# Eight transfers instead of three in a loop that this data never enters, and where the last store's semaphore comes to lie

## The chip, the core and the metric

The kernel runs on one core of a Trainium2 chip. TensorE (PE) multiplies matrices into PSUM and takes its weights on a track of its own (PEld); VectorE (DVE) and ScalarE (ACT) work element by element; GpSimd (POOL) does some copies and issues the software transfers; SyncE (SP) computes nothing and issues transfers and waits. The engines run apart and meet at semaphores. The metric is the device time of one execution in microseconds.

## The reference

```python
scores = scale * np.matmul(q, k.transpose(0, 1, 3, 2))      # batch 8, 8 heads, 576 positions, 64 wide
mask = (rel >= 0) & (rel < window)                           # window 64, causal
attn = softmax(np.where(mask, scores, -1000000000.0))
x = matmul(attn, v), heads side by side                      # 4608 tokens x 512
out = (silu(x @ w_gate) * (x @ w_val)) @ w_out               # 512 -> 1536 -> 512
```

Each position sees itself and the 63 before it. The attention's output goes straight into a gated feed-forward block.

## The kernel before

The 4608 tokens are worked in nine tiles of 512. A tile is the first 512 positions of one batch; the eighth tile gathers the last 64 positions of all eight batches. For each tile the kernel computes scores, their exponentials and the sums, mixes the values, scales into `xT`, runs twelve slices of gate and value products into `hT` (`gate_value`, L469), and projects `hT` in four parts of 128 tokens (`project_part`, L479). The order is written out by hand: the tile framework here only places the semaphores, so each engine's instructions come in the order of the source. The projections of one tile are woven between the attention of the next.

This fast path leaves out the maximum in the softmax. That is right as long as no sum gets out of bounds, so it gathers evidence as it goes: `survey` (L542) and `tally` (L549) count the partitions whose sums stayed in range into `count`. Near the end (L984) every engine loads that number as `good`, and behind it stands a general path for the data that the fast path can't do:

```python
with tc.If(good < P, preferred_fallthrough_block=True):      # L990
    set_exp()
    with tc.For_i(0, 8 * H, 1) as i:                         # L992
        general_attention(i)
    set_silu()
    with tc.For_i(0, NTOK // P, 1) as i:                     # L995
        general_ffn(i)
project(NT - 1, 2, bank[4])                                  # L997
project_last(NT - 1, 3)                                      # L998
```

The first loop does the attention of one head of one batch per turn, the second the feed-forward block for 128 tokens per turn. They write all of the output anew. Parts 0 and 1 of the last tile are projected ahead of the `If`, parts 2 and 3 behind it. With the data given here all sums stay in range, `good` is 128, and both loops are skipped.

Three things matter around the change:

Behind the `If` SyncE issues three stores: part 2 of the last tile (`project_end`, L513, 256 KB), and part 3 in two pieces of 384 and 128 columns (`project_last`, L540, 192 KB and 64 KB). The 64 KB store is the last of the kernel. Before, these three have hardware semaphores 0, 1 and 2.

## Time and profile before

| | us |
|---|---|
| median of 3 runs | 322.56 (322.48 to 322.86) |
| profiled execution | 322.44 |
| its span, first to last instruction | 320.6 |
| granted TensorE clock | 1.000 |
| TensorE busy | 315.5 (98%) |
| last store issued | 317.66 to 318.05 |

The span runs from the program's first instruction to its last; 1.84 us of the execution's time lie around it. A share of 98% for TensorE means that elsewhere only the ends, where TensorE has not begun or is done, are open to change. In answers on a line, an instruction of an engine's sequencer (a semaphore wait, a branch, a drain) carries a `q` behind the engine's name; such an answer gives the count, the shortest, median and longest duration in nanoseconds, and the starts of the first and the last in microseconds.

### The profile page before, as it was taken

What the parts mean: (1) busy time and instruction counts of PE and PEld (TensorE: products, weight loads), DVE (VectorE), ACT (ScalarE), POOL (GpSimd) and SP (SyncE); (2) the same over time, 40 slices, a digit from 0 to 9 for tenths busy, and PEclk for the clock granted to TensorE, in tenths of its full rate; (3) what the DMA queues carried; (4) which work ended last, traced back from release to release, by engine and by line L of the source; (5) the groups of instructions that cost most, each with busy time, mean ns of one, the idle gap of its engine ahead of it and who ended that gap; (6) DMA issues with size and microseconds to landing.
All of it is one profiled execution on the core that took longest, in us unless ns stands there. A gap on an engine that the chain in (4) does not pass through costs nothing. (4 is left out here: it accounts for less than half of the span.)

```text
span 320.6 us, 8214 instructions
## 1 busy us (share of the span) xinstructions
PE 315.5 (98%) x3298; PEld 154.8 (48%) x3298; DVE 214.4 (67%) x349; ACT 208.7 (65%) x327; POOL 147.4 (46%) x268
## 2 busy tenths in 40 slices
PE   8999999999999999999999999999999999999995
PEld 3544444445444644455445544554446444644443
DVE  5879846497576847685688667866786576843431
ACT  5967665768565875688477946694667665875600
POOL 4965657767566235741751099408765300000000
PEclk9999999999999999999999999999999999999999
DMA  7999999999799449983994369629998400021012
GB/s 250 203 196 198 207 151 226 207 197 123 155 194 182 48 108 173 199 88 99 163 195 52 81 110 116 70 54 141 184 187 104 109 0 0 4 82 52 1 37 99
DMA packets 83529, 40.45 MB, mean 126 GB/s; under 512 B 64160, under 2 KB 78752, under 8 KB 83488
## 3 DMA queue, kind: packets, MB, share of 16 engines
q0 software_dynamic: 51488, 22.59, 58.6%
q1 hardware_dynamic: 31456, 16.79, 22.6%
q8 instruction: 26, 0.43, 0.6%
q10 hardware_dynamic: 544, 0.52, 0.5%
q14 instruction: 15, 0.12, 0.1%
HBM read 53.02 MB, written 9.44 MB: 195 GB/s over the span
## 5 line engine op out<-in xcount | busy, mean ns | idle before, releaser
L466 ACT ACTIVATE sg<-one 128x512 f32<-128x512 f32 x107 | 63.9, 597 | 80.6 <-PE one L473 67.8
L467 DVE TENSOR_TENSOR hT<-sg,one 128x512 bf16<-128x512 f32 x107 | 74.0, 692 | 57.4 <-PE one L473 53.8
L473 PE MATMUL one<-xT,wg 128*128 128x512 bf16 x416 | 106.8, 379 | 0.0
L473 PE MATMUL one<-xT,wv 128*128 128x512 bf16 x416 | 106.8, 379 | 0.0
L142 POOL DMA_DIRECT2D k_s<-in_k_dram x112 | 60.4, 560 | 27.0 <-DMA q_s<-in_q_dram 13.1
L473 PEld LDWEIGHTS <-wv 128*128 128x128 bf16 x416 | 40.7, 98 | 49.1
L473 PEld LDWEIGHTS <-wg 128*128 128x128 bf16 x416 | 40.6, 98 | 48.8
L482 PE MATMUL one<-wo,hT 128*128 128x512 bf16 x252 | 56.6, 380 | 0.1
L958 POOL COPY past<-xT 128x1 bf16<-128x1 bf16 x8 | 1.5, 189 | 87.6 <-DVE xT L430 87.5
L494 PE MATMUL one<-wo,hT 64*64 64x512 bf16 x672 | 40.0, 377 | 0.0
L482 PEld LDWEIGHTS <-hT 128*128 128x128 bf16 x252 | 23.7, 98 | 29.7 <-issue 2.6
L430 DVE TENSOR_TENSOR xT<-two,r 128x512 bf16<-128x512 f32 x34 | 21.3, 684 | 23.0 <-ACT r L353 23.0
L233 DVE STREAM_TRANSPOSE kT<-k_s 128x512 bf16<-128x512 bf16 x28 | 36.1, 1290 | 0.0
L755 ACT ACTIVATE eb<-eb 128x960 bf16<-128x960 bf16 (+1 forms) x32 | 32.1, 1002 | 0.0
L308 ACT ACTIVATE eb<-two 128x960 bf16<-128x960 f32 (+1 forms) x32 | 29.5, 974 | 3.0 <-PE two L293 2.9
L494 PEld LDWEIGHTS <-hT 64*64 64x64 bf16 x672 | 18.6, 107 | 13.6
L313 DVE TENSOR_TENSOR eb<-eb,mask 128x960 bf16<-128x960 bf16 (+1 forms) x32 | 20.9, 655 | 5.8 <-ACT eb L308 5.8
L223 DVE STREAM_TRANSPOSE qT<-q_s 128x512 bf16<-128x512 bf16 x32 | 22.2, 700 | 0.1
L353 ACT ACTIVATE r<-r 128x1024 f32<-128x1024 f32 (+1 forms) x20 | 19.2, 968 | 0.1
L318 DVE TENSOR_TENSOR both<-eb 128x512 bf16<-128x512 bf16 x32 | 13.6, 425 | 1.1
L168 POOL DMA_DIRECT2D vb<-in_v_dram x16 | 11.0, 701 | 6.6 <-DMA wo<-in_moe_w_out_dram 3.8
L107 POOL DMA_DIRECT2D q_s<-in_q_dram x24 | 13.0, 552 | 2.0 <-DMA v<-in_v_dram 1.3
(149 smaller groups left out, 273.1 us busy)
## 6 DMA issues: line engine op xcount, KB each, us to landing
k_s<-in_k_dram POOLq DMA_DIRECT2D x112, 56.0 KB, 5.2
q_s<-in_q_dram POOLq DMA_DIRECT2D x24, 248.0 KB, 6.2
v_f<-in_v_dram SPq DMA_DIRECT2D x40, 128.0 KB
wg<-in_moe_w_gate_dram POOLq DMA_DIRECT2D x5, 256.0 KB, 8.3
wv<-in_moe_w_val_dram POOLq DMA_DIRECT2D x5, 256.0 KB, 8.9
q_f<-in_q_dram SPq DMA_DIRECT2D x4, 256.0 KB
wo<-in_moe_w_out_dram POOLq DMA_DIRECT2D x2, 512.0 KB, 10.7
vb<-in_v_dram POOLq DMA_DIRECT2D x16, 64.0 KB, 6.5
```

The costliest lines, as they stand in the source:

```text
L142: nc.gpsimd.dma_start(k_s[p0:p0 + 32, g, :, 0:w], k[b, a:H:2, s:s + P].rearrange("u (r e) d -> r u (e d)", e=4) [:, :, 32 * c:32 * c + w],)
L223: nc.vector.transpose(queries[t][:, u, :].rearrange("r (e x) -> r e x", e=16), staged[t][0][:, u].rearrange("r (e d) -> r e d", d=D)[:, :, ...
L233: nc.vector.transpose(dst[:, u, :].rearrange("r (g x e) -> r g e x", g=4, e=4), k_s[:, :, u].rearrange("r g (e d) -> r g e d", d=D)[:, :, ...
L308: nc.scalar.activation(flat, s_ps[:].rearrange("r a b -> r (a b)")[:, 0:n], AF.Exp, scale=0.125)
L313: nc.vector.tensor_mul(flat, flat, mask[:].rearrange("r j c e y -> r (j c e y)")[:, 0:n])
L430: nc.vector.tensor_mul(x, o_ps, r)
L466: nc.scalar.activation(sg[:], g_ps[:], AF.Silu)
L467: nc.vector.tensor_mul(hT[t][:, m, :], sg[:], v_ps[:])
L473: nc.tensor.matmul(ps[:], w[:, c, P * m:P * m + P], xT[t][:, c, :], start=(c == 0), stop=(c == 3),)
L482: nc.tensor.matmul(o_ps[:], hT[t][:, c, P * s:P * s + P], wo[:, c, :], start=(c == 0), stop=(c == 11),)
L494: nc.tensor.matmul(tiles[s][half(y)], hT[t][half(x), c, r0:r0 + 64], wo[half(x), c, :], start=not back and c == 0, stop=bool(back) and c = ...
L755: nc.scalar.activation(flat, flat, AF.Copy, accum_out=extent())
```

## The change

In `general_ffn`, the body of the second loop, the load of `x_b` is cut into four, one for each 128 rows of `x_all`, and each of the two stores is cut into two halves of the columns. That makes eight transfers on ScalarE's queue in the loop's text instead of three. What they move is the same. The semaphores are handed on from there: the three stores behind the `If` have hardware semaphores 5, 6 and 7 instead of 0, 1 and 2, so that the last has the eighth.

```diff
@@ general_ffn
         x_b = att.tile([P, 4, P], BF16, name="x_b", tag="xT")
-        nc.scalar.dma_start(
-            x_b[:], x_all[:, bass.ds(i * P, P)].rearrange("(c r) s -> r c s", r=P)
-        )
+        for c in range(4):
+            nc.scalar.dma_start(x_b[:, c], x_all[P * c:P * c + P, bass.ds(i * P, P)])
@@
         nc.scalar.copy(os_[:], bank[4])
-        nc.scalar.dma_start(out[bass.ds((i * P + NTOK - 64) % NTOK, 64)], os_[0:64])
-        nc.scalar.dma_start(out[bass.ds(i * P, 64)], os_[64:P])
+        ahead = (i * P + NTOK - 64) % NTOK
+        for f in (slice(0, 256), slice(256, 512)):
+            nc.scalar.dma_start(out[bass.ds(ahead, 64), f], os_[0:64, f])
+            nc.scalar.dma_start(out[bass.ds(i * P, 64), f], os_[64:P, f])
```

In the built program this changes, on the path that is executed: the amounts that the eight steps of the branch add (32 for all eight semaphores, where five had 16), the semaphores of the three stores, the number of waits ahead of the first of them on SyncE (three instructions instead of two), and the thresholds of the epilogue's waits. In the skipped part, SyncE's text has 12 instructions more and ScalarE's ten more.

Lines behind the loop body (from L664 on) are numbered one higher in the changed kernel: the `If` is L991, the epilogue L1024.

## The prediction

> **What bounds the kernel now.** I read the page first, for the engine shares and the chain, then the timeline of SyncE over the last microseconds, then the instructions of the epilogue's line and of the `If`'s line, and last the instruction packets. The page's head says that TensorE is the bound, and nowhere else can much be won or lost:

> ```profile
> PE 315.5 (98%) x3298; PEld 154.8 (48%) x3298; DVE 214.4 (67%) x349; ACT 208.7 (65%) x327; POOL 147.4 (46%) x268
> ```

> The lines of the changed loop (L632 to L663) have no instruction in the trace: the data are tame, `good` is 128, and every engine takes the branch over both loops. So the added transfers are never issued. What is left of the change is what the built program does with it on the executed path. The built programs agree instruction for instruction, semaphore and threshold up to the `If`; they differ only in the skipped second loop and in SyncE's tail behind the `If`. I therefore read that tail.

> The timeline of SyncE (start, duration, line, the store):

> ```profile
> 315.42 0.35 SPq L513 DMA_DIRECT2D out_dram<-os__4885  x1
> 317.24 0.81 SPq L540 DMA_DIRECT2D out_dram<-os__4888  x2
> ```

> The instructions of L1023 (the epilogue) on SyncE, asked of four short windows in order of time (count, min/median/max ns, first and last start):

> ```profile
> L1023 SPq EVENT_SEMAPHORE  x5: 17/28/28, 318.1 to 318.3; - x5
> ...
> L1023 SPq EVENT_SEMAPHORE  x1: 28/28/28, 319.2 to 319.2; - x1
> ...
> L1023 SPq EVENT_SEMAPHORE  x1: 28/28/28, 319.4 to 319.4; - x1
> ...
> L1023 SPq EVENT_SEMAPHORE  x5: 28/28/28, 319.4 to 319.7; - x5
> ```

> And the same line's drains, which come behind those waits, with SyncE's waits in the stretch from 318 to 321 us:

> ```profile
> L1023 SPq DRAIN  x2: 7/7/7, 319.7 to 319.8; - x2
> ```
> ```profile
> SPq L1023 <- DMA out_dram<-os__4888: 1.0, 2, 0.8
> ```

> Here is the epilogue. SyncE waits for the transfer queues' semaphores one instruction after another, in a fixed order: the eight software ones, paired, then hardware 0, 1, 2 ... 7, then a drain, then the barrier. There are twelve such waits. Before, the three stores behind the `If` carry hardware semaphores 0, 1 and 2. The first five waits pass at once (318.1 to 318.3; the fifth holds hardware 0). The sixth (hardware 1, the 192 KB store) is answered at 319.2, the seventh (hardware 2, the 64 KB store, the kernel's last) at 319.4. Then hardware 3 to 7 are still to be read, though they were full long ago: five waits, 319.4 to 319.7, and only then the drain. The reader should see that these five stand behind the last landing, on the path that ends the kernel.

> The other engines do not set the barrier:

> ```profile
> L1023 POOLq DRAIN  x1: 2682/2682/2682, 306.8 to 306.8; - x1
> L1023 ACTq DRAIN  x1: 8/8/8, 306.8 to 306.8; - x1
> L1023 PEldq DRAIN  x1: 1835/1835/1835, 315.4 to 315.4; - x1
> L1023 DVEq DRAIN  x1: 330/330/330, 317.3 to 317.3; - x1
> ```

> All four are drained by 317.6 us (317.3 + 0.33), 2.1 us before SyncE arrives.

> **The change part by part.**

> *The order of the hardware semaphores.* The three stores behind the `If` move from semaphores 0, 1, 2 to 5, 6, 7. The twelve waits stay, in the same order. Hardware 0 to 5 now pass while the two last stores are still on their way; hardware 6 is answered at 319.2, hardware 7 at 319.4, and the drain follows at once. So five waits leave the path. One costs 0.06 us from start to start: four such steps lie between 318.1 and 318.3, and five waits and the step to the drain fill 319.4 to 319.7. Bounds: the busy time alone is 5 x 28 ns = 0.14 us; by the rounded starts the stretch is at most 0.4 us. I take 5 x 0.06 = 0.30 us, the middle of the stretch itself. Moving five waits ahead of the landing costs nothing while they fit in the 0.8 us that SyncE waited there: 5 x 0.06 = 0.30 us, so 0.5 us of cover remains.

> [...]

> *One wait more ahead of the 256 KB store (L513).* SyncE's waits there go from two to three instructions, because that store now follows five semaphores instead of three. All are already full. They are covered:

> ```profile
> L990 SPq EVENT_SEMAPHORE  x4: 17/17/17, 314.7 to 314.9; - x4
> L513 SPq EVENT_SEMAPHORE  x2: 17/22/28, 315.0 to 315.0; - x2
> ```

> The store itself starts at 315.42, held by VectorE's copy of the same tile (314.70 + 0.69 = 315.39). One more step of 0.06 ends near 315.1, with 0.3 us to spare. Without that cover it would cost 0.06 us on this store alone, and the next store starts at 317.24, held by VectorE again (316.65 + 0.56 = 317.21). So nothing either way.

> *The eight semaphore steps on the branch not taken into the loops (L990).* They add 32 instead of 16 for five semaphores; same instructions, same waits. The fifth waits for the 256 KB store issued at 312.47 (answered at 314.7) before and after. Nothing.

> *Longer skipped code.* SyncE skips 12 instructions more (five in the block for no iteration, seven at the loop's back edge), ScalarE ten more; TensorE, VectorE and GpSimd skip what they did. Fetched code is a rival below. In the sum it is nothing: ScalarE's step behind the branch starts at 306.7, and TensorE, which waits for it, gets there at 311.83, 5.1 us later; SyncE's branch at 312.9 is followed by four waits from 313.1 to 313.4 and then by 1.3 us of waiting for the landing at 314.7. A delay of a microsecond at either branch would be swallowed.

> *Sum.* Profiled execution: 322.44 us (span 320.6, 1.84 around it) - 0.30 = 322.14. That execution stands 0.12 under the median of the three runs, 322.56; against the median: 322.56 - 0.30 = **322.26 us**, 0.09% less. About 0.2% (0.65 us) is what a measurement of this kernel can tell from no change, so by that bound this is no change: even the upper bound of 0.4 us stays inside, and the lower, 0.14, gives 322.42.

> **The rivals.**

> *Slower: a code boundary comes to lie in the tail.* The longer skip moves SyncE's last 35 instructions 12 places on. Code comes in packets on the instruction queues:

> ```profile
> q8 instruction: 26, 0.43, 0.6%
> ...
> q14 instruction: 15, 0.12, 0.1%
> ```

> A packet of q14 takes about 0.001 x 16 x 320.6 / 15 = 0.34 us (0.2 to 0.5 by the rounding), of q8 about 1.2. In a window of 306 to 309 us, 40 slices of 0.075 us, the packets stand at 307.3 and 308.8:

> ```profile
> DMA  0000000000000000070000000000000000000900
> ```

> That is 1.1 us behind the branches of ScalarE and GpSimd (306.2) and of TensorE (307.7). So a stall for code would be up to 1.1 + 0.34 = 1.4 us. It decides only where the boundary falls among the instructions behind the last landing: the drains and the two barrier steps. Then the time is 322.26 + 1.4 = 323.7 (for a packet alone 322.6). Ahead of 319.2 the wait for the stores covers it. Against it: all streams cross such boundaries some forty times (26 + 15 packets), TensorE is 98% busy through its own, and SyncE's first step behind its taken branch comes 0.2 us later (312.9 to 313.1), so the target was there already. For it: I can't see where SyncE's boundary lies. [...] Chance 0.12.

> *Nothing won: the barrier is held by something other than SyncE's arrival.* Then 322.56. Against it: the four drains above are over by 317.6, and the barrier's steps follow SyncE's drain at 319.8 directly. Chance 0.10.

> *The two last stores land in the other order.* The 64 KB store could be answered first; then one wait stays behind the last landing, and 4 x 0.06 = 0.24 is won: 322.32. It lands in the likeliest case's own range, and I count it there.

> *Faster by more.* The mirror of the first: the stall for code lies today behind the last instruction, within the 1.84 us outside the span, and goes: 322.26 - 1.4 = 320.9. No row shows such a stall. Chance 0.08.

> *The change doesn't do what it says.* That would need the last store on another semaphore; the built program puts it on the eighth. Excluded.

> **How the numbers follow.** Likeliest (0.70): 322.26, between 322.42 and 322.16 by the bounds, give or take the runs' own spread of about 0.2 (322.48 to 322.86). Nothing won 0.10, boundary 0.12, faster by more 0.08. The range holds the first two with that spread, 321.9 to 322.8, and leaves the other two out. Within 0.2%: 0.70 + 0.10 = 0.80. Slower 0.12, faster 0.08.

> **What would show it.** In the trace of the changed kernel: SyncE's twelve epilogue waits with ten of them started by 318.7, one at about 319.2 and one at about 319.4, and the first drain right behind at about 319.4 instead of 319.7; three waits of L513 behind the branch, with the store still at 315.4; a span of 320.3. The L540 stores should start at 317.2 as before. The prediction is wrong if the waits behind the last landing are still five, if the gap comes back between drain and barrier, or if a packet of q14 stands ahead of a gap on SyncE behind 319.4.

## The result, and the profile after

The changed kernel takes 322.10 us in the median of 22 runs (321.62 to 323.15), the kernel before 322.71 us in 22 runs beside it (322.21 to 327.71). The ratio is 0.9982, with a 95% interval of 0.9976 to 0.9989: 0.58 us less, between 0.36 and 0.77. By the bound of 0.2% that is no change, but it is clear of zero, and it is about twice the 0.30 us that the prediction worked out. The run of 327.71 us is a slow one and does not enter the ratio; the next highest is 323.27. Two more measurements of the same kernel gave 0.9983 (0.9973 to 0.9992) and 0.9978 (0.9962 to 0.9993).

The profiled execution fell from 322.44 to 321.98 us, so by 0.46: its span from 320.6 to 320.3 (0.34 by the trace's own ends, 320.615 and 320.275), and what lies around it from 1.82 to 1.71.

SyncE's timeline of the changed kernel (start, duration, line, store); the last row holds both L540 stores. They start where they did before, 317.23 against 317.24:

```profile
315.45 0.36 SPq L513 DMA_DIRECT2D out_dram<-os__4890  x1
317.23 0.81 SPq L540 DMA_DIRECT2D out_dram<-os__4893  x2
```

The epilogue's line on SyncE, now L1024, asked of four short windows in order of time (count, shortest/median/longest ns, first and last start), and the drains:

```profile
L1024 SPq EVENT_SEMAPHORE  x8: 17/28/28, 318.1 to 318.6; - x8
...
L1024 SPq EVENT_SEMAPHORE  x2: 28/28/28, 319.0 to 319.0; - x2
...
L1024 SPq EVENT_SEMAPHORE  x1: 28/28/28, 319.1 to 319.1; - x1
...
L1024 SPq EVENT_SEMAPHORE  x1: 28/28/28, 319.3 to 319.3; - x1
...
L1024 SPq DRAIN  x2: 7/7/7, 319.4 to 319.5; - x2
```

The five waits that stood between the last landing and the drain are gone: the wait for hardware 7 is answered at 319.3 and the drain follows at 319.4, where it was 319.4 and 319.7. So far it is as forecast. One thing is not. Ten waits should have been through by 318.7. Only eight are: between the waits for hardware 3 and 4 SyncE pauses, from 318.58 to 318.97 by the trace's starts, 0.39 us where a step takes 0.06. Nothing was left to wait for there: hardware 4 was already read full by the step of the branch at 315.0, and ScalarE's semaphore, which shares that wait, last changed at 306.2. The pause lies under the landing of the last stores; the run with four transfers below has the same tail without it (3.03 us against 3.04), so here it costs nothing. About a microsecond after its beginning, 0.6 us after its end, an instruction packet moves. The answer on transfers for 319 to 320.2 us (40 slices of 0.03 us, then the queue) has it at 319.6; the same stretch of the kernel before has none:

```profile
DMA  0000000000000000000800000000000000000000
...
q14 instruction: 1, 0.01, 2.2%
```

I read this as a boundary of SyncE's code that has come into the tail, with a pause of its own, but in front of the last landing. That it is one is inferred from the packet; the trace shows the pause and the packet alone. That raised two questions: is the gain of the span the semaphores' alone, and what makes up the rest of the 0.58 us?

### The profile page after: what moved, and what is told of

Its sections match the earlier page's. It is cut to its first block, busy times and chain, and to the rows that moved or that the text cites. A ratio compares the mean times of both kernels' runs of the same rounds, so it can differ in the third digit from the quotient of the medians.

```text
span 320.3 us, 8184 instructions
## 1 busy us (share of the span) xinstructions
PE 313.0 (98%) x3267; PEld 154.7 (48%) x3298; DVE 214.2 (67%) x349; ACT 208.7 (65%) x327; POOL 147.4 (46%) x268
## 5 line engine op out<-in xcount | busy, mean ns | idle before, releaser
L473 PE MATMUL one<-xT,wg 128*128 128x512 bf16 x405 | 104.7, 379 | 0.1
L482 PE MATMUL one<-wo,hT 128*128 128x512 bf16 x241 | 55.5, 379 | 0.9 <-issue 0.3
```

The lines of the kernel that those rows point to most:

```text
L473: nc.tensor.matmul(ps[:], w[:, c, P * m:P * m + P], xT[t][:, c, :], start=(c == 0), stop=(c == 3),)
L482: nc.tensor.matmul(o_ps[:], hT[t][:, c, P * s:P * s + P], wo[:, c, :], start=(c == 0), stop=(c == 11),)
```

## The experiments

Theory A: only the order of the semaphores counts (0.3 us in the span). Theory B: in addition the pause, taken to belong to a boundary of SyncE's code and to lie behind the span in the kernel before, is now covered. Three numbers serve throughout. The *tail* is the time from the start of the first L540 store to the end of the span; it leaves out where an execution stood when it got there, which differs by up to a microsecond from one to the next. *Outside* is a run's time less its span, over all runs of a kernel. The *boundary* is the instruction of SyncE's text at which the changed kernel pauses, found again by counting SyncE's instructions in the built programs.

| kernel | last three stores on | boundary | tail, us | outside, us: mean (lowest to highest) | median against before, us |
|---|---|---|---|---|---|
| before | 0, 1, 2 | 4 behind the end | 3.38 | 1.90 (1.68 to 2.10) | |
| changed | 5, 6, 7 | under the landing | 3.04 | 1.71 (1.68 to 1.75) | -0.61 |
| four transfers | 5, 6, 7 | 3 behind the end | 3.03 | 1.76 (1.68 to 1.91) | -0.35 |
| eleven | 0, 1, 2 | behind the landing | 3.75 | 1.71 (1.68 to 1.79) | +0.27 |
| boundary at a drain | 5, 6, 7 | behind the landing | 3.48 | 1.62 (1.58 to 1.65) | -0.19 |
| changed again | 5, 6, 7 | under the landing | 3.04 | 1.75 (1.69 to 1.78) | -0.68 |
| boundary only | 0, 1, 2 | ahead of the stores | 3.39 | 1.70 (1.66 to 1.76) | -0.25 |
| far, by GpSimd | 5, 6, 7 | 10 behind the end | 3.04 | 1.49 (1.44 to 1.52) | -0.59 |
| far, without the small loads | 5, 6, 7 | 10 behind the end | 3.04 | 1.72 (1.66 to 1.76) | -0.50 |

The first four experiments were compared with 35 runs of the kernel before (median 322.83, its outside the 1.90 of the table), the next four with 35 others (323.02, outside 1.94), the last four with 35 more (322.91, outside 1.95).

### Four transfers: the semaphores alone

```diff
-        nc.scalar.dma_start(x_b[:], ...)          # one load
+        for c0, c1 in ((0, 2), (2, 4)):
+            nc.scalar.dma_start(x_b[:, c0:c1], ...)
```

> Four transfers in the skipped loop: the load is cut into two, the stores stay whole. The three stores behind the If get hardware semaphores 5, 6 and 7 as in the changed kernel, but SyncE's text is only one instruction longer than before (the changed kernel: 13). Theory A, only the order of the semaphores counts: the same gain in the span as the changed kernel, 320.6 to 320.3 us, and about 0.3 to 0.35 us less time than before. Theory B, the changed kernel gained in addition because a boundary of SyncE's code moved from behind its last instruction to a place under the stores' landing: the span falls by the same 0.34, but the time outside the span stays at 1.82 us (the changed kernel: 1.71), so the time is 0.1 us above the changed kernel's, and no pause of 0.3 us stands between two of the epilogue's waits.

322.48 us, ratio 0.9989 (0.9978 to 1.0). SyncE's epilogue, in windows as above:

```profile
317.55 0.81 SPq L540 DMA_DIRECT2D out_dram<-os__4889  x2
...
L1024 SPq EVENT_SEMAPHORE  x10: 17/28/28, 318.4 to 318.9; - x10
...
L1024 SPq EVENT_SEMAPHORE  x1: 28/28/28, 319.5 to 319.5; - x1
...
L1024 SPq EVENT_SEMAPHORE  x1: 28/28/28, 319.6 to 319.6; - x1
...
L1024 SPq DRAIN  x2: 7/7/7, 319.7 to 319.8; - x2
```

Ten waits run through without a pause, then two landings, then the drain: this is the epilogue as the prediction drew it. The tail is the changed kernel's, 3.03. That settles the first question: the 0.34 us of the span come from the order of the semaphores, without the longer text. Outside lies between before and changed, 1.76 on average, with single runs up to 1.91; theory B expected 1.82. What the trace shows of this stands with the boundary alone, below.

The build shows one more thing. The text ahead of the prediction says that the framework hands out the semaphores in turn. It isn't quite so: with four, five, seven, eight and twelve transfers the last store gets the eighth semaphore, with three and eleven the third.

### Eleven transfers: the longer text with the old semaphores

```diff
-        nc.scalar.dma_start(x_b[:], ...)          # load in three pieces
-        ... two stores ...                        # each in four pieces of 128 columns
+        for c0, c1 in ((0, 2), (2, 3), (3, 4)): ...
+        for f in [slice(128 * n, 128 * n + 128) for n in range(4)]: ...
```

> Eleven transfers in the skipped loop (load in three, stores in four pieces each): the three stores have hardware semaphores 0, 1 and 2 again as before, while SyncE's text is 12 longer, about as in the changed kernel. Theory A: the five waits are behind the last landing again and nothing else changes: time as before, span 320.6. Theory B: the boundary of SyncE's code now falls on the epilogue's wait for hardware 5, behind the last landing: a pause of 0.3 to 0.4 us there, uncovered; span 320.95, outside 1.71, time 0.2 to 0.3 us above before. If the changed kernel's gain came from the longer text and not from the semaphores, this one would gain too: 0.3 to 0.5 us less than before.

323.10 us, ratio 1.0008 (0.9997 to 1.0019): by the times alone unclear, but the trace isn't:

```profile
L1026 SPq EVENT_SEMAPHORE  x1: 28/28/28, 320.0 to 320.0; - x1
...
L1026 SPq EVENT_SEMAPHORE  x2: 28/28/28, 320.1 to 320.1; - x2
...
L1026 SPq EVENT_SEMAPHORE  x3: 28/28/28, 320.5 to 320.7; - x3
...
L1026 SPq DRAIN  x2: 7/7/7, 320.7 to 320.8; - x2
```

The last store is answered at 320.0 (hardware 2). Two waits later SyncE pauses, from 320.15 to 320.53, and then takes the three others. It pauses before the wait for hardware 5, as the count of instructions said. The five waits and the pause now both stand behind the landing, and the tail is 3.75: 0.37 above before. So this is what the slower rival would have cost: 0.33 us for the pause (0.39 less one step), 0.37 with the slower steps beside it, not 1.4.

### The boundary behind the landing, with the new semaphores

```diff
-        nc.scalar.dma_start(x_all[...], x_h[0:D])             # first loop, two stores
-        nc.scalar.dma_start(x_all[...], x_h[0:D, S - 64:S])
+        nc.gpsimd.dma_start(x_all[...], x_h[0:D])
+        nc.gpsimd.dma_start(x_all[...], x_h[0:D, S - 64:S])   # and ten transfers in the second
```

> Ten transfers in the second loop and, in the first, the two stores moved from ScalarE's queue to GpSimd's: the stores behind the If keep semaphores 5, 6 and 7 as in the changed kernel, but SyncE's text is five shorter than the changed kernel's, so that the instruction at which the changed kernel paused (the epilogue's wait for hardware 4) is now the second drain, behind the last landing. Theory A: as the changed kernel, span 320.3, 0.3 to 0.45 us less than before. Theory B: the pause of 0.3 to 0.4 us comes behind the landing: span 320.6, time 0.1 us under before at most.

322.64 us, ratio 0.9997 (0.9985 to 1.0008). The last landing, the first drain and the second:

```profile
L1026 SPq EVENT_SEMAPHORE  x1: 28/28/28, 319.5 to 319.5; - x1
...
L1026 SPq DRAIN  x1: 7/7/7, 319.6 to 319.6; - x1
...
L1026 SPq DRAIN  x1: 123/123/123, 319.9 to 319.9; - x1
```

The pause has moved with the count to the second drain, which starts 0.36 us behind the first (0.06 before) and takes 0.12 more by itself. The tail is 3.48, 0.44 above the changed kernel's. The tail's gain is more than lost, though the semaphores are the changed kernel's. Theory A alone falls here. The transfers on GpSimd's queue are no rival cause: the run far by GpSimd, below, has such transfers too, and there the second drain follows the first after 0.06 us. That the pause stays at one place of the text, whether a wait or a drain stands there, is shown by this run, the one with eleven transfers and the changed kernel. That it has to do with the fetching of code is inferred, from the instruction packet that starts 1.0 us after the pause begins in each of the three. By then the pause has been over for 0.6 us, so it is no wait for that packet; what SyncE does in it isn't shown.

### The changed kernel beside them

> The changed kernel again, beside the others on one chip. Both theories: span 320.3, 0.35 to 0.6 us less than before, ten of the twelve epilogue waits started ahead of the last landing, a pause of 0.3 us between the waits for hardware 3 and 4 that the landing covers.

322.15 us, ratio 0.9983. Tail 3.04, pause between the waits for hardware 3 and 4, as in its first profile.

### The boundary alone

```diff
-            nc.scalar.dma_start(out[bass.ds(i * P, 64), f], os_[64:P, f])
+            nc.sync.dma_start(out[bass.ds(i * P, 64), f], os_[64:P, f])   # the kernel with eleven
```

> Eleven transfers in the skipped loop, four of them issued by SyncE instead of ScalarE: the stores behind the If have hardware semaphores 0, 1 and 2 as before, but SyncE's text is 27 longer, so that the boundary of its code falls on the third wait ahead of the 256 KB store (315.1 us), where TensorE's work covers a pause. Theory B, in two parts: the span stays as before (five waits behind the last landing, 2.95 us from the last store's issue to the end), and the time outside the span, 1.90 us on average in the runs of the kernel before and between 1.68 and 2.10, falls to 1.7 with little spread; time 0.2 us under before. Theory A, semaphores alone: time as before, outside still 1.9. The other rival, that the part outside the span has to do with the semaphores: outside still 1.9 too.

322.77 us against 323.02; the ratio's interval, 0.9977 to 1.0003, just holds no change. The steps of the branch (L993 here), the last landing with the five waits behind it, and the drain:

```profile
L993 SPq EVENT_SEMAPHORE  x1: 17/17/17, 315.1 to 315.1; - x1
...
L993 SPq EVENT_SEMAPHORE  x3: 17/17/17, 315.5 to 315.6; - x3
...
L1026 SPq EVENT_SEMAPHORE  x1: 28/28/28, 319.7 to 319.7; - x1
...
L1026 SPq EVENT_SEMAPHORE  x5: 28/28/28, 319.8 to 320.0; - x5
...
L1026 SPq DRAIN  x1: 7/7/7, 320.1 to 320.1; - x1
```

The pause lies at 315.1 to 315.5, six instructions ahead of where I had counted it, probably because SyncE's transfers in the loop take more instructions than the count showed. It holds up the 256 KB store, which is issued 1.59 us ahead of the first L540 store where the kernel before has 1.82, but not the L540 stores. The tail is 3.39, against 3.38 before: five waits behind the landing. And outside falls from 1.94 to 1.70, with no run above 1.76. So the second part of the gain, 0.2 us, has nothing to do with the semaphores. It goes with the longer text, and so, as I read it, with the boundary, which by the count lay four instructions behind the end of the span before.

The traces fit that place, but don't show how it costs the time. Only two of them have a packet of q14 that starts behind the span's end: the one with four transfers, at 322.20 us, and the kernel before, at 322.41. This is the answer on transfers for 320 to 324 us of the kernel before (40 slices of 0.1 us, then the queue):

```profile
DMA  0000000000000000000000002000000000000000
...
q14 instruction: 1, 0.01, 0.5%
```

Counted back by the 1.0 us of the other runs (an estimate), SyncE crossed 0.6 and 0.8 us behind the end. There the traces have only the times at which semaphores are set, the last of them 1.90 us behind the end in the kernel before. With four transfers one block of them (207 to 255) is set 0.3 to 0.4 us later than in the kernel before and the last one 0.04 later; that would fit a pause that is covered for the most part, and an outside of 1.76. In the kernel before all these times agree with the changed kernel's to 0.03 us. What its 0.2 us are spent on stays open.

### The boundary far behind the end

```diff
-        nc.scalar.dma_start(...)      # the second loop's three transfers
+        nc.gpsimd.dma_start(...)
```

> The three transfers of the skipped second loop go through GpSimd's queue: stores behind the If on semaphores 5, 6 and 7, SyncE's text six shorter than before, so the boundary of its code lies ten instructions behind the program's end instead of four. Theory B: the tail in the span as in the changed kernel (2.6 us from the last store's issue to the end), the time outside 1.7 to 1.9, since the boundary still lies there; time 0.3 to 0.5 us under before. If the pause is covered by something at that place, outside is 1.7 and the time equals the changed kernel's.

322.43 us, ratio 0.998 (0.9967 to 0.9993); tail 3.04. Outside is 1.49, lower than expected, but the spans are longer than a tail of 3.04 explains: 321.05 on average, where the kernel before had 321.14 with a tail of 3.38. Two runs asked why.

```diff
-            nc.gpsimd.tensor_mul(h_b[...], sg, val)                    # on the changed kernel
+            for f in range(0, 512, 64):
+                nc.gpsimd.tensor_mul(h_b[...][:, :, f:f + 64], sg[:, :, f:f + 64], val[:, :, f:f + 64])
```

> The changed kernel with GpSimd's two products in the skipped second loop cut into sixteen: GpSimd's text is 14 instructions longer, SyncE's is that of the changed kernel. It asks why the time outside the span was 1.49 us in the run with SyncE's boundary far behind the end, and 1.62 in the run with the boundary among the drains: both also had 15 or 16 instructions more on GpSimd. If GpSimd's text decides: outside 1.5 to 1.6 here, 0.1 to 0.2 us under the changed kernel's time. If SyncE's alone decides: outside 1.71 to 1.75 as in the changed kernel.

322.17 us, ratio 0.997 (0.9954 to 0.9986), outside 1.73 (1.67 to 1.77), tail 3.06: the changed kernel's. GpSimd's text doesn't decide it.

```diff
-            if lead:                                  # on the kernel before, first loop
-                nc.scalar.dma_start(f[64:P, 0], ...)
-            else:
-                nc.scalar.dma_start(f[0:64, 4], ...)
```

> The kernel before without the three small loads of the first loop (the general path's edges of q, k and v are left out; that path isn't taken): the stores behind the If have semaphores 5, 6 and 7, SyncE's boundary lies ten instructions behind the end as in the run with GpSimd's transfers, and GpSimd's text is 3 shorter than before. If SyncE's text decides: outside 1.49, last issue to end 2.61 to 2.65, time 0.6 to 0.8 us under before. If GpSimd's text decides: outside 1.7, or 1.9 if the pause is still uncovered at that place.

322.41 us, ratio 0.9983 (0.9968 to 0.9998), outside 1.72, tail 3.04. With the boundary, by the count, ten instructions behind the end, outside is no longer than when it is covered (1.71 in the changed kernel beside it). In this trace and in that of the run far by GpSimd the last packet of q14 starts at 312.80 and 314.31 us, beside SyncE's branch, so no row shows that SyncE reaches the boundary at all. SyncE's text doesn't bring 1.49 either.

> The kernel whose second loop's three transfers go through GpSimd, again, beside the changed kernel: tail and outside as in its first run (2.62 and 1.49 us), which is 0.2 us less than the changed kernel has in the two together. If its long span in the first run (profiled 321.6, mean 321.05) was the chance of its loads, the time is now 0.7 us under before and 0.2 under the changed kernel; if it belongs to the kernel, again about 0.5 under before.

322.27 us, ratio 0.9982 (0.9965 to 1.0), outside 1.49 again, mean span 321.04; the changed kernel in the same comparison has 1.71 and 320.75. So the 1.49 is real, but it saves nothing, since the span is longer: the mean times are 322.53 and 322.46. It may be that the span's ends lie elsewhere; no run shows it. What the 1.49 and the 1.62 of the run with the boundary at a drain have in common is that transfers of the loops go through GpSimd's queue. Why that shifts 0.1 to 0.2 us stays open.

> The changed kernel once more, as the measure for the other three: outside 1.71 to 1.75, last issue to end 2.61, 0.55 us under before, give or take 0.3.

322.40 us, ratio 0.9978; tail 3.04, outside 1.71.

### The last stores on two queues

```diff
-            nc.sync.dma_start(out[r0:r0 + P, f0:f1], os_[:, f0:f1])
+            (nc.scalar if f0 else nc.sync).dma_start(out[r0:r0 + P, f0:f1], os_[:, f0:f1])
```

> The changed kernel with its last store (64 KB) issued by ScalarE, which has nothing to do there, instead of SyncE, which is busy with the 192 KB store's issue from 317.23 to 317.56. The issue can start when VectorE's copy ends (317.55) instead of at 317.67, so at most 0.1 us is won, if ScalarE issues as fast as SyncE (0.38 us). Both theories: 0 to 0.1 us under the changed kernel, 0.5 to 0.7 under before.

322.35 us, ratio 0.9976 (0.9963 to 0.9989), tail 3.04. ScalarE issues the 64 KB store at 317.31 where SyncE would have come to it 0.1 us later, but it is answered 1.75 us after its issue instead of 1.66. Nothing won.

> The changed kernel with the 192 KB store on ScalarE's queue and the last store on SyncE's, which is then free: the last store's issue starts at 317.6 instead of 317.67, 0 to 0.1 us under the changed kernel. If ScalarE issues more slowly or the two queues' packets meet on the transfer engines, the 192 KB store lands later than the last and nothing is won or up to 0.2 lost.

The same edit the other way round, the 192 KB store on ScalarE: 322.23 us, ratio 0.9976 (0.9964 to 0.9987), tail 3.10. The last store starts 0.03 us behind VectorE's copy instead of 0.11, and is answered 1.80 us after its issue. Nothing won either: no version here beats the changed kernel by more than these measurements tell apart.

## Why the prediction was right, and where it was not

The forecast, no change by the bound of 0.2%, came true, and a little over half of the gain came by the mechanism that it named. The rest, some 0.2 us, was not in the sum. 322.10 us lies below the bounds that were worked out, 322.16 to 322.42, and is in the range only by the width given for the spread of the runs.

- **The order of the semaphores, 0.30 us.** Right in mechanism and size. The span lost 0.34 in the profile, the tail 3.38 to 3.04; the run with four transfers has it without anything else. Of the 0.34, 0.30 are the five waits; the landing was also answered 0.05 us sooner after its issue (1.66 against 1.71).
- **One wait more ahead of the 256 KB store, nothing.** Right in cost, but the cover was thinner than worked out. In the profile of after the 256 KB store issued at 312.46 was answered at 315.0 instead of 314.7, the three waits ended at 315.41, and the next store started at 315.45, 0.03 later than before. The L540 stores start at 317.23.

```profile
L513 SPq EVENT_SEMAPHORE  x3: 17/28/28, 315.3 to 315.4; - x3
```

- **Longer skipped code, nothing.** The step that failed. "Fetched code is a rival below. In the sum it is nothing": it belonged in the sum with a gain of 0.2 us. The kernel before has the boundary behind its span, and outside 1.90 us on average with runs from 1.68 to 2.10; the changed kernel has it under the landing, and outside 1.71. The run with the boundary alone shows this part by itself, 1.94 to 1.70. That the place of the boundary decides is inferred from these times and from where the packets lie; how it costs the 0.2 us isn't shown. The sum against the profile was 322.44 - 0.30; with this term it is 0.34 + 0.2 = 0.54 us less, and 0.58 was measured.
- **The slower rival.** The pause is real and its place was all that kept it from deciding: it did come into the tail, 0.4 us ahead of the last landing. Its price was mis-sized. I took 1.4 us from the distance between a branch and its packet; the runs with the boundary behind the landing show 0.37 (eleven against before) and 0.44 (at a drain against changed), and the pause doesn't wait for the packet.
- **The rival of a larger gain** named the right place, behind the last instruction, with the same wrong size: 1.4 instead of 0.2. "No row shows such a stall" still holds, but the trace on hand did show a packet of q14 there, at 322.41 us, behind the stretch that the prediction shows; the 0.2 us show only in time less span over many runs.
- **Nothing won** and **another semaphore for the last store** are both excluded by the drain at 319.4. A packet of q14 does stand at 319.6, ahead of SyncE's last step in the barrier, but that step comes 0.51 us behind the one before it in both kernels: the named sign of a slower change is not there.

Where the pause lay ahead of a wait for a landing or of a wait for VectorE's copy, the tail didn't grow: 3.04 us in the changed kernel against 3.03 without it, 3.39 with the boundary alone against 3.38 before. In a row of waits that pass at once, the step across it takes 0.39 us instead of 0.06.

## What to carry to other kernels

At the end of a program whose epilogue reads the queues' semaphores one by one, put the last transfer on the one that is read last: each wait behind it cost 0.06 us here, and the five 0.30. Text that is never executed still counted, since it placed the semaphores and the pause in what comes after it; look for a pause between two instructions that have nothing to wait for, and lengthen or shorten the skipped text until it lies under a wait: behind the last landing it cost 0.37 and 0.44 us of tail here, under a wait none. For a question of 0.1% compare a stretch of the trace that begins at the change, not whole executions: here the tail repeats to 0.03 us while the same kernel's times spread over more than a microsecond.

## What was not expected of the hardware

A pause of 0.3 to 0.4 us on SyncE at one place of its text (in the changed kernel 318.58 to 318.97), with an 8 KB packet on the second instruction queue (0.13 MB in 16 packets in the changed kernel's span) 1.0 us after its beginning, when the pause has been over for 0.6 us (the changed kernel and the two runs with the pause behind the landing). In the changed kernel the steps shortly ahead of it are slower too, 0.07 to 0.09 us instead of 0.06. And the last store of 64 KB is answered later after its issue, 1.75 and 1.80 us instead of 1.66, when the two last stores are issued from two engines than when SyncE issues both.
